# Two layers of dilated local attention and a bilinear GLU: own places for the first chunks' q, k and v, wo loaded directly, and an order planned from other durations

## The chip, the cores and the metric

The kernel runs on one core of a Trainium2 chip. The metric is device time in microseconds of the whole program on that core, so lower is better. The engines have the names of the profile: PE is the matrix engine (TensorE; PEld is its weight load), DVE is VectorE, ACT is ScalarE, POOL is GpSimd, and SP is SyncE, which only issues DMAs here. Everything between them is ordered by semaphores, and each engine works through its own list in order.

## The reference

```python
def _A_ref(x, wqkv, wo):                       # B, S, D = 1, 2048, 576
    H = 32; Dh = D // H                        # 18 values a head
    W, dil = 8, 2
    q, k, v = (x @ wqkv) ...                   # [B, H, S, Dh] each
    idx = pos[:, None] - arange(W) * dil       # the token itself and 7 earlier ones
    logits = einsum("bhsd,bhswd->bhsw", q, k[idx]) * Dh ** -0.5   # -1e9 where idx < 0
    o = einsum("bhsw,bhswd->bhsd", softmax(logits), v[idx])
    return o.reshape(B, S, D) @ wo

def _B_ref(x, w_gate, w_up, w_down):           # F = 4608
    return ((x @ w_gate) * (x @ w_up)) @ w_down

x = x + _A_ref(_layernorm(x), A_wqkv, A_wo)
x = x + _B_ref(_layernorm(x), B_w_gate, B_w_up, B_w_down)
x = x + _A_ref(_layernorm(x), A_wqkv, A_wo)    # the same weights again
x = x + _B_ref(_layernorm(x), B_w_gate, B_w_up, B_w_down)
```

## The kernel before

**Chunks.** The 2048 tokens are 16 tiles of 128. A chunk is one or two tiles that go through one attention and one GLU. There are 18 chunks: first layer pair, tiles 0, 1, 2, 3 one by one (chunks 0 to 3), tiles 4-5 and 6-7 (chunks 4 and 5), second layer pair for tiles 0 to 7 (chunks 6 to 9), then the same for tiles 8 to 15 in pairs (chunks 10 to 17). Chunk 0 is called "fast" in the code and takes shorter ways.

**One attention** (`attention`): `head` makes a layernorm: statistics on DVE (L343, L344), the inverse root as Ln and Exp on ACT (L349, L350), the application on ACT (L358; L359 writes the last 64 columns a second time), and a transpose, on PE through a PSUM bank with a copy on ACT (L369, L372) for chunks 0 to 4, by DMA (L362) for the others. `project` multiplies by `wqkv` on PE (L407) into one pair of PSUM banks after another, and ACT (for chunk 0 partly DVE) moves q, k and v to `qT`, `kT`, `vT` (L460, L477, L484, L449). These have two places, taken in turn by odd and even chunks. k and v have 14 columns of the chunk before in front, the halo, copied by ACT (L392, L453 in, L489 out). DVE multiplies q by two shifts of k at a time (L503) and adds up (L507, L511, L512), PE sums over the head's values with `Esel` (L518), DVE and ACT make the softmax (L540 to L551). The weights are spread over the partitions: for chunks 0 to 4 by four matmuls with `Bsel` (L557), each copied out of PSUM; for the others through `a_dram` in DRAM (L567, L570). DVE multiplies v by them, shift by shift, and adds (L587, L602); PE multiplies by `wo` (L614), DVE adds the residual (L620), and a second `head` gives `xnT_B`, of which there are three.

**One GLU** (`glu`): PE makes 512 columns of gate and up in a pair of PSUM banks (L655, and L666 for the last 64 rows), ACT copies gate (L677), DVE multiplies it by up (L678), and after half of F (a third for a single tile) PE multiplies by `w_down` (L699, L700) and DVE adds into `xf` (L709, L714). `wd` slices of `w_down` come through six buffers, loaded anew for each chunk by SP.

**What sets the order.** All of this is entered as operations of a `Plan`: an engine, a cost in ns, keys read and written, a priority. `Plan.run` takes, at each step and over all engines, the operation that can start earliest by these costs (the priority decides only between equals), and issues it. The result is a fixed list for each engine. A key that is written waits for all earlier readers in the order of entry. `LAT` is added where a result goes to another engine, `margin` where a step on PE waits for another engine. DMA time is counted as bytes at 250 per ns plus 2000 ns. PE's work for attention stands in the same list as the GLU's matmuls.

**The start.** `load_x`, `setup_a`, `setup_b`, `setup_wo` and `setup_glu` enter the loads, all on SP. `wqkv` is put into another order of columns by DVE and ACT (L292, L294). `wo` is copied within DRAM first (L318), then loaded from there (L320, L323). Until chunk 0 is through its attention, its small steps use the third pair of PSUM banks and `acct`; later ones have the one bank `pa`.

Of the kernel before, what the change touches and what calls it, by code (L numbers as in the profile page):

```python
# [15 lines left out]
class Op:  # L16
    __slots__ = ("eng", "cost", "fn", "deps", "order", "succ", "n", "prio", "idx", "hold", "free",
                 "lat", "margin", "ready", "end", "nbytes", "use", "pair", "need")


class Plan:
# [4 lines left out]
    LAT = {"PE": 250, "ACT": 130, "DVE": 110, "POOL": 150, "SP": 0}  # L26
# [6 lines left out]
    def op(self, eng, cost, fn, r=(), w=(), prio=1, after=None, hold=None, free=None, margin=0, nbytes=0, use=None,  # L33
           pair=None, need=None):
        o = Op()
        o.eng, o.cost, o.fn, o.prio, o.hold, o.free = eng, cost, fn, prio, hold, free
# [32 lines left out]
    def run(self, slots):  # L69
        clock = {e: 0.0 for e in self.LAT}  # L70
        dma = 0.0
# [3 lines left out]
        while cand:  # L75
            best = None
            for o in cand:
                t = 0.0
                for p in o.deps:
                    e = p.ready if p.eng != o.eng else p.end  # L80
                    if e > t:
                        t = e
                t += o.margin
                if o.hold is not None:
                    f = free[o.hold]
                    if not f:
                        continue
                    t = max(t, min(f)[0])
                if o.pair is not None:
                    if len(free["unit"]) < len(o.pair):  # L90
                        continue
                    t = max(t, min(free["unit"])[0])
# [21 lines left out]
            if o.nbytes:  # L114
                dma = max(dma, o.end) + o.nbytes / 250.0
                o.ready = dma + 2000
# [16 lines left out]
def kernel(  # L133
# [44 lines left out]
    wo_dram = dram.tile([D, D], BF16, name="wo_dram")  # L178
# [13 lines left out]
    xf = [sb(f"xf{i}", [P, NST, D], FP32) for i in range(NXS)]  # L192
# [9 lines left out]
    xnT_B = [sb(f"xnT_B{i}", [P, KT, CH]) for i in range(NXB)]  # L202
    qT_ = [sb(f"qT{i}", [P, KT, CH]) for i in range(2)]
    kT_ = [sb(f"kT{i}", [P, KT, HALO + CH]) for i in range(2)]
    vT_ = [sb(f"vT{i}", [P, KT, HALO + CH]) for i in range(2)]
    oT = sb("oT", [P, KT, CH])
    n_al = nlayers // 2
    halo_k = [sb(f"halo_k{i}", [P, KT, HALO]) for i in range(n_al)]
    halo_v = [sb(f"halo_v{i}", [P, KT, HALO]) for i in range(n_al)]
# [46 lines left out]
    def load_x(t0, nst):  # L256
        b, i0 = (t0 // 2) % 2, t0 % 2
        op("SP", 600, dma(xb[b][:, i0:i0 + nst, :], xv[:, t0:t0 + nst, :]), w=[f"xb{b}_{i}" for i in range(i0, i0 + nst)],
           nbytes=P * nst * D * 2, prio=1.5 if t0 else 0)
# [13 lines left out]
    def setup_b():  # L273
        def mk_zero():
            for t_ in qT_ + kT_ + vT_:
                nc.gpsimd.memset(t_[TL:P, KF, :], 0.0)
            for t_ in halo_k + halo_v:
                nc.gpsimd.memset(t_[:], 0.0)
        op("POOL", 1500, mk_zero, w=[f"{x}{t}{i}" for x in "qkv" for t in (4, "H") for i in range(2)] + [f"halo{x}{i}" for x in "kv" for i in range(n_al)])
        for k in range(KT):  # L280
            for t3 in (0, 1, 2, 3):
                if t3 < 3:
                    src = wraw[:, k, t3 * D:(t3 + 1) * D].rearrange("p (h d) -> p d h", h=H)[:, 0:16, :]
                    dst = wqkv[:, k, t3 * 512:(t3 + 1) * 512].rearrange("p (d h) -> p d h", h=H)
                    cost = (615, 1080)
                else:
                    src = wraw[:, k, :].rearrange("p (t h d) -> p t d h", t=3, h=H)[:, :, 16:18, :]
                    dst = wqkv[:, k, 3 * 512:3 * D].rearrange("p (t d h) -> p t d h", t=3, h=H)
                    cost = (280, 500)
                rk = [f"wraw{k}"] if k < KF else ["wrawt0", f"wrawt{TL}"]  # L290
                if t3 % 2 == 0:
                    op("DVE", cost[0], lambda dst=dst, src=src: nc.vector.tensor_copy(dst, src), r=rk, w=[f"wq{t3}_{k}"], prio=2)  # L292
                else:
# [10 lines left out]
        op("POOL", 9000, mk_sel, w=["sel"])  # L304
# [12 lines left out]
    def setup_wo():  # L317
        op("SP", 600, dma(wo_dram[:].rearrange("(d h) n -> h d n", h=H), A_wo.rearrange("(h d) n -> h d n", d=Dh)),  # L318
           w=["wod"], nbytes=D * D * 2, prio=2)
        op("SP", 600, lambda: nc.sync.dma_start(wo_p[:, 0:KF, :], wo_dram[0:KF * P, :].rearrange("(t p) n -> p t n", p=P)),  # L320
           r=["wod"], w=["wo0"], nbytes=KF * P * D * 2, prio=2)
        for r_ in (0, TL):
            op("SP", 600, lambda r_=r_: nc.sync.dma_start(wo_p[r_:r_ + TL, KF, :], wo_dram[KF * P:D, :]),  # L323
               r=["wod"], w=[f"wot{r_}"], nbytes=TL * D * 2, prio=2)
# [11 lines left out]
    def head(src, keys, nst, dst, key, prio, ab, on_pe, mg):  # L336

        mv, st, rstd, nmr, xn = mv_[ab], st_[ab], rstd_[ab], nmr_[ab], xn_[ab]
        for i in range(nst):
            def stats(i=i):  # L340
                xr = src(i).rearrange("p (a b) -> p a b", a=2)
                for a in range(2):
                    nc.vector.bn_stats(out=st[:, i, a, :], in_=xr[:, a, :])  # L343
                nc.vector.bn_aggr(out=mv[:, i, :], in_=st[:, i])  # L344
            op("DVE", 1070, stats, r=[keys[i]], w=[f"mv{ab}{i}"], prio=prio)
        mk = [f"mv{ab}{i}" for i in range(nst)]

        def rs():
            nc.scalar.activation(rstd[:, 0:nst], mv[:, 0:nst, 1], ACT.Ln, bias=eps_t[:])  # L349
            nc.scalar.activation(rstd[:, 0:nst], rstd[:, 0:nst], ACT.Exp, scale=-0.5)  # L350
        op("ACT", 490, rs, r=mk + ["eps"], w=[f"rstd{ab}"], prio=prio)
        op("DVE", 210, lambda: nc.vector.scalar_tensor_tensor(nmr[:, 0:nst], mv[:, 0:nst, 0], -1.0, rstd[:, 0:nst],
                                                              op0=ALU.mult, op1=ALU.mult),
           r=mk + [f"rstd{ab}"], w=[f"nmr{ab}"], prio=prio)
        for i in range(nst):
            def apply(i=i):
                x = src(i)
                nc.scalar.activation(xn[i][:, 0:D], x, ACT.Identity, bias=nmr[:, i:i + 1], scale=rstd[:, i:i + 1])  # L358
                nc.scalar.activation(xn[i][:, D:D + TL], x[:, KF * P:D], ACT.Identity, bias=nmr[:, i:i + 1], scale=rstd[:, i:i + 1])  # L359
            op("ACT", 1300, apply, r=[keys[i], f"nmr{ab}", f"rstd{ab}"], w=[f"xn{ab}{i}"], prio=prio)  # L360
            if not on_pe:
                op("SP", 900, lambda i=i: nc.sync.dma_start_transpose(out=dst[:, :, i * P:(i + 1) * P], in_=xn[i][:]),  # L362
                   r=[f"xn{ab}{i}"], w=[key + str(i)], prio=0, nbytes=P * KT * P * 2)
# [3 lines left out]
            def tr(i=i, b=b):  # L367
                for k in range(KT):
                    nc.tensor.transpose(bf(b())[:, k, :], xn[i][:, k * P:(k + 1) * P], ident[:])  # L369
            o = op("PE", 290, tr, r=[f"xn{ab}{i}", "ident"], prio=0, margin=mg, **b.take())  # L370
            pl.also(o, [key + str(i)])
            op("ACT", 700, lambda i=i, b=b: nc.scalar.copy(dst[:, :, i * P:(i + 1) * P], bf(b())), r=[b.key], w=[key + str(i)],  # L372
# [4 lines left out]

    def attention(j, la, t0, nst):
        fast = j == 0
        z = j % 2  # L380
        qT, kT, vT = qT_[z], kT_[z], vT_[z]
# [8 lines left out]
        xk = [f"xA{i}" for i in range(nst)]  # L390
        head(lambda i: xin[:, i0 + i, :], xin_k, nst, xnT_A, "xA", prio, 0, on_pe, mg)
        op("ACT", 250, lambda: nc.scalar.copy(kT[:, :, 0:HALO], halo_k[la][:]), r=[f"halok{la}"], w=[f"kH{z}"], prio=prio)  # L392
# [4 lines left out]
        def project(tag, au, bu, tl, ea, eb, dkeys):  # L397
# [7 lines left out]
            def mm(u, part, k, r_, start, stop):  # L405
                p_, e, c0, m = part
                nc.tensor.matmul(bank(p_, u)[0:m, e * n:(e + 1) * n], lhsT=wqkv[r_, k, c0:c0 + m], rhs=xnT_A[r_, k, 0:n],  # L407
# [45 lines left out]
        op("ACT", 250, lambda: nc.scalar.copy(vT[:, :, 0:HALO], halo_v[la][:]), r=[f"halov{la}"], w=[f"vH{z}"], prio=prio)  # L453
        mpb = 4 // nst
        if nst == 2:
# [3 lines left out]
            def ev_q(m):  # L459
                return (600, lambda u, d: nc.scalar.mul(qT[:, 2 * m:2 * m + 2, 0:n], grp(0, u, 2), qscale), [f"q{2 * m}{z}"], 0)  # L460

            def ev_k(m):
                return (590, lambda u, d: cp(d, kT[:, 2 * m:2 * m + 2, HALO:HALO + n], grp(1, u, 2)), [f"k{2 * m}{z}"], 0)

            project("q", un[0], un[1], tq, [ev_q(0), ev_k(0)], [ev_q(1), ev_k(1)], [f"{x}{z}" for x in ("q0", "k0", "q2", "k2")])
# [3 lines left out]
            tb, vs = 0, slice(0, n)  # L469
        else:  # L470
# [3 lines left out]
            tb, vs = 1, slice(n, 2 * n)  # L474
            tq = [(h_, 0, uq[4 * h_ + e]) for e in range(4) for h_ in range(2)]
            tq += [(0, 1, uv[0]), (1, 1, ut[0]), (0, 1, uv[1]), (1, 1, ut[1]), (0, 1, uv[2]), (0, 1, uv[3])]
        ev_t = [(390, lambda u, d: nc.scalar.mul(qT[0:TL, KF, 0:n], bank(tb, u)[0:TL, 0:n], qscale), [f"q4{z}"], 0),  # L477
                (390, lambda u, d: cp(d, kT[0:TL, KF, HALO:HALO + n], bank(tb, u)[TL:P, 0:n]), [f"k4{z}"], 1),
                (390, lambda u, d: cp(d, vT[0:TL, KF, HALO:HALO + n], bank(1, u)[TL:P, vs]), [f"v4{z}"], 0)]
        if nst == 2:  # L480
            ev_v = [(590, lambda u, d, m=m: cp(d, vT[:, 2 * m:2 * m + 2, HALO:HALO + n], grp(m, u, 2)), [f"v{2 * m}{z}"], 0) for m in range(2)]
            project("v", ut, uv, tv, ev_t, ev_v, [f"{x}{z}" for x in ("v0", "v2", "q4", "k4", "v4")])
        else:
            ev_a = [(600, lambda u, d: nc.scalar.mul(qT[:, 0:KF, 0:n], grp(0, u, 4), qscale), [f"q0{z}", f"q2{z}"], 0),  # L484
                    (590, lambda u, d: cp(d, kT[:, 0:KF, HALO:HALO + n], grp(1, u, 4)), [f"k0{z}", f"k2{z}"], 1)]
# [309 lines left out]
```

## Time and profile before

| | us |
|---|---|
| median of three runs | 1096.06 |
| lowest and highest | 1095.94, 1097.07 |
| the profiled execution, its run | 1094.6 |
| its span in the profile | 1092.5 |
| PE busy | 1057.1 |
| DVE busy | 761.4 |
| ACT busy | 364.1 |
| POOL busy | 5.9 |

The granted clock of PE is 0.991 over the span. The profile lists for each group of instructions its line, engine, operation, tiles, count and mean time; the views by stage give busy time between two moments. Busy times on one engine are of overlapping instructions where they are pipelined, so the time from start to start is the better price of one among many. A few records of matmuls are missing.

### The profile page before, as it was taken

The page shows a single profiled execution, that of the slowest core. Times are in us where ns is not written, and L with a number is a line of the kernel's source. Part 1 is how long each engine was busy: PE and PEld are TensorE (multiplying, and loading weights), DVE is VectorE, ACT ScalarE, POOL GpSimd, SP SyncE. Part 2 cuts the span into 40 slices and gives each one's busy share as a digit, 9 for nine tenths or more (in the row PEclk, how much of TensorE's full clock was granted, in tenths as well). Part 3 has the DMA queues.
Part 4 walks back from the last instruction along what each step waited for, and adds up shares of the span by engine and source line. Part 5 has one row for each costly group of instructions (what it writes and reads, how often), then busy time and mean ns, then how long its engine had stood idle before and what let it go on. Part 6 is the DMA issues. An engine that isn't in the chain of part 4 may idle for free.

```text
span 1092.5 us, 25296 instructions
## 1 busy us (share of the span) xinstructions
PE 1057.1 (97%) x10812; PEld 792.8 (73%) x10812; DVE 761.4 (70%) x1347; ACT 364.1 (33%) x768; POOL 5.9 (1%) x26
## 2 busy tenths in 40 slices
PE   5889999999999999999999899999999999999998
PEld 4668887777777777777767677777787777777775
DVE  6688889697979868798978563785757867322222
ACT  7435254432244443323342222314242232211111
POOL 2000000000000000000000000000000000000000
PEclk9899999999999999999999999999999999999999
DMA  8954563633333532535361434342333323333331
GB/s 261 336 155 119 172 200 98 183 110 97 95 99 102 147 84 74 135 112 155 99 168 24 122 99 122 92 121 56 117 106 122 107 72 121 105 96 109 116 110 55
DMA packets 146239, 133.17 MB, mean 122 GB/s; under 512 B 42000, under 2 KB 145488, under 8 KB 146128
## 3 DMA queue, kind: packets, MB, share of 16 engines
q1 hardware_dynamic: 146128, 131.57, 41.9%
q8 instruction: 84, 1.38, 0.5%
q14 instruction: 27, 0.22, 0.1%
HBM read 118.96 MB, written 4.73 MB: 113 GB/s over the span
## 4 chain that ended last, share of the span: by engine, by line
PE 88%; DVE 5%; DMA 4%; SPq 1%; issue 1%; ACT 1%; DVEq 0%; ACTq 0%
PE pu L655 21%; PE pg L655 21%; PE pg L699 12%; PE pu L699 10%; PE pg L666 6%; PE pg L407 6%; PE pu L407 4%; PE pa L614 3%; PE acct L700 3%; DMA a_dram<-s 2%; DMA ab<-a_dram 1%; SPq L570 1%; DMA wraw<-in_A_wqkv_dram 1%; DVE h L678 1%; DVE prod L503 1%
## 5 line engine op out<-in xcount | busy, mean ns | idle before, releaser
L677 ACT CAST g_sb<-pg 128x512 bf16<-128x512 f32 x288 | 158.9, 586 | 493.6 <-PE pu L666 359.7
L655 PE MATMUL pg<-xnT_B,wg 128*128 128x256 bf16 (+1 forms) x2592 | 301.1, 262 | 1.1 <-ACT xnT_B L372 1.1
L655 PE MATMUL pu<-xnT_B,wu 128*128 128x256 bf16 (+1 forms) x2592 | 301.9, 262 | 0.1
L678 DVE TENSOR_TENSOR h<-pu,g_sb 128x512 bf16<-128x512 f32 x288 | 193.3, 684 | 130.6 <-ACT g_sb L677 74.8
L655 PEld LDWEIGHTS <-wu 128*128 128x128 bf16 x2592 | 225.2, 98 | 40.1 <-issue 16.5
L655 PEld LDWEIGHTS <-wg 128*128 128x128 bf16 x2592 | 230.2, 98 | 28.9 <-issue 1.5
L699 PE MATMUL pg<-wd,h 128*128 128x512 bf16 x648 | 231.9, 382 | 0.0
L700 PE MATMUL acct<-wd,h 128*128 128x64 bf16 x1152 | 222.4, 193 | 0.0
L699 PEld LDWEIGHTS <-h 128*128 128x128 bf16 x1152 | 113.0, 98 | 130.5 <-issue 1.1
L699 PE MATMUL pu<-wd,h 128*128 128x512 bf16 x504 | 191.5, 380 | 0.9 <-DVE h L678 0.9
L587 DVE TENSOR_TENSOR prod<-vT,ab 128x1280 bf16<-128x1280 bf16 (+1 forms) x127 | 94.0, 741 | 47.1 <-DMA ab<-a_dram 46.0
L407 PEld LDWEIGHTS <-wqkv 128*128 128x128 bf16 (+1 forms) x1260 | 98.7, 99 | 25.6 <-issue 14.5
L700 PEld LDWEIGHTS <-h 128*128 128x128 bf16 x1152 | 113.1, 98 | 2.1 <-issue 1.1
L503 DVE TENSOR_TENSOR prod<-qT,kT 128x2560 bf16<-128x2560 bf16 (+1 forms) x72 | 95.7, 1332 | 22.4 <-ACT kT L449 21.9
L602 DVE TENSOR_TENSOR oT<-oT,prod 128x1280 bf16<-128x1280 bf16 (+1 forms) x119 | 90.8, 763 | 3.2
L666 PE MATMUL pu<-xnT_B,wgu_t 64*128 64x256 bf16 (+1 forms) x648 | 79.7, 259 | 4.2 <-DVE h L678 4.2
L407 PE MATMUL pg<-xnT_A,wqkv 128*128 128x256 bf16 (+3 forms) x650 | 79.7, 265 | 2.5 <-ACT xnT_A L372 1.6
L666 PE MATMUL pg<-xnT_B,wgu_t 64*128 64x256 bf16 (+1 forms) x648 | 79.8, 259 | 0.0
L407 PE MATMUL pu<-xnT_A,wqkv 128*128 128x256 bf16 (+3 forms) x610 | 77.2, 266 | 0.1
L709 DVE TENSOR_TENSOR xf<-pg,xf 128x512 f32<-128x512 f32 (+1 forms) x40 | 27.4, 684 | 66.3 <-PE pg L699 58.4
L666 PEld LDWEIGHTS <-wgu_t 64*128 64x128 bf16 x1296 | 50.3, 94 | 27.8 <-issue 22.6
L614 PE MATMUL pa<-wo_p,oT 128*128 128x288 bf16 x310 | 48.2, 286 | 2.5 <-DVE oT L602 1.8
(91 smaller groups left out, 614.0 us busy)
## 6 DMA issues: line engine op xcount, KB each, us to landing
wd<-in_B_w_down_dram SPq DMA_DIRECT2D x324, 288.0 KB, 3.4
ab<-a_dram SPq DMA_DIRECT2D x52, 128.0 KB, 2.7
wg<-in_B_w_gate_dram SPq DMA_DIRECT2D x6, 768.0 KB, 9.4
wu<-in_B_w_up_dram SPq DMA_DIRECT2D x6, 768.0 KB, 10.7
out_dram<-xf SPq DMA_DIRECT2D x8, 288.0 KB, 5.4
wraw<-in_A_wqkv_dram SPq DMA_DIRECT2D x4, 432.0 KB, 5.5
xb<-in_A_x_dram SPq DMA_DIRECT2D x6, 288.0 KB, 4.6
a_dram<-s SPq DMA_DIRECT2D x13, 128.0 KB, 2.2
```

Of the source, the lines that this page charges most:

```text
L407: nc.tensor.matmul(bank(p_, u)[0:m, e * n:(e + 1) * n], lhsT=wqkv[r_, k, c0:c0 + m], rhs=xnT_A[r_, k, 0:n], start=start, stop=stop, skip_g ...
L503: nc.vector.tensor_tensor(late["prod"][p_ % 2][:, :, :, 0:n], q2, k2, op=ALU.mult)
L587: nc.vector.tensor_tensor(js(dst), js(vT[:, :, o0:o0 + n]), abw, op=ALU.mult)
L602: op("DVE", 60 + 3 * n, lambda i_=i_: nc.vector.tensor_tensor(oT[:, :, 0:n], oT[:, :, 0:n], late["prod"][i_ % 2][:, 0, :, 0:n], op=ALU.add ...
L614: nc.tensor.matmul(b()[:, 0:HD], lhsT=oT[:, t, i * P:(i + 1) * P], rhs=wo_p[:, t, hh * HD:(hh + 1) * HD], start=(t == 0), stop=(t == KT - 1))
L655: nc.tensor.matmul(pt[:, e * n:(e + 1) * n], lhsT=w_[:, k, ft * P:(ft + 1) * P], rhs=xT[:, k, 0:n], start=(first and k == 0 and e == 0), s ...
L666: nc.tensor.matmul(ps[:, e * n:(e + 1) * n], lhsT=wgu_t[r_, ft * P:(ft + 1) * P], rhs=xT[r_, KF, 0:n], start=(first and e == 0), stop=not ...
L677: op("ACT", 590, lambda: nc.scalar.copy(g_sb[gs][:, 0:ul], pg[use["slot"]][:, 0:ul]), r=[f"wg_{j}_{u}"], w=[f"g{gs}"], prio=0)
L678: op("DVE", 690, lambda: nc.vector.tensor_tensor(hb[hs][:, 0:ul], pu[use["slot"]][:, 0:ul], g_sb[gs][:, 0:ul], op=ALU.mult), r=[f"wu_{j}_{ ...
L699: nc.tensor.matmul((pg, pu)[i][use["slot"]][:], lhsT=lhs, rhs=wt[:, e % 2, 0:512], start=first, stop=fin)
L700: nc.tensor.matmul(acct[:, i * TL:(i + 1) * TL], lhsT=lhs, rhs=wt[:, e % 2, 512:D], start=(first and i == 0), stop=fin, skip_group_check=True)
L709: op("DVE", 690, lambda i=i, dst=dst: nc.vector.tensor_tensor(dst[:, 0:512], (pg, pu)[i][use["slot"]][:], xs_f[:, i0 + i, 0:512], op=ALU.add),
```

## The change

It has these parts; all loads stay on SP's queue (`first` is always true).

1. q, k and v of the first five chunks have places of their own: the single tiles are the halves of the two existing places, chunk 4 lies in the part of `xf` that holds tiles 4 to 7 later. `xnT_A` and the layernorm's small tiles are also used by halves. k and v are one tile `kv_`, so the halo takes one copy in and one out.
2. x of tiles 4 and 5 is loaded once more, early, into a half of `xf[1]`, and chunk 4's first layernorm reads it there; it is entered with chunk 3.
3. `wo` is loaded straight from its input, in six DMAs of 32 partitions.
4. The reordering of `wqkv` is shared by DVE, ACT and POOL.
5. For transposes on PE the second application (L359) goes, and the last 64 columns are transposed twice. For single tiles two matmuls with `Bsel` share a bank and one copy. Chunk 0's small k and v evacuations are one.
6. Nearly all costs of the plan have other values, and the plan has new rules: a GLU evacuation that is due goes first if another operation would hold it up by more than `SLACK`; a margin also counts after a bank comes free; the landing of transposes and of the spread weights is put later.

```diff
+SLACK = {"DVE": 500, "ACT": 300}
-    LAT = {"PE": 250, "ACT": 130, "DVE": 110, "POOL": 150, "SP": 0}
+    LAT = {"PE": 250, "ACT": 150, "DVE": 150, "POOL": 150, "SP": 0}
...
-                    t = max(t, min(f)[0])
+                    t = max(t, min(f)[0] + o.margin)
...
+                if o.due and (o.eng not in urgent or key < urgent[o.eng][0]):
+                    urgent[o.eng] = (key, o)
+            o = best[1]
+            if not o.due and o.eng in urgent and urgent[o.eng][0][0] < best[0][0] + o.cost - SLACK[o.eng]:
+                best = urgent[o.eng]
...
-                o.ready = dma + 2000
+                o.ready = dma[o.eng] + 2000 + o.late
...
+    xtmp = xf[1][:, 1].bitcast(BF16).rearrange("p (i d) -> p i d", i=NST)
...
-                if t3 % 2 == 0:
+                if t3 == 0 or t3 == 3:
                     op("DVE", cost[0], ... nc.vector.tensor_copy(dst, src) ...)
+                elif t3 == 2:
+                    op("POOL", 1000, ... nc.gpsimd.tensor_copy(dst, src) ...)
...
-        op("SP", 600, dma(wo_dram[:].rearrange("(d h) n -> h d n", h=H), ...
+        for dd in range(4):
+            op("SP", 470, dma(wo_p[32 * dd:32 * dd + 32, 0:KF, :], wv_[:, dd:16:4, :]), ...)
+        for dd in range(2):
+            op("SP", 470, dma(wo_p[32 * dd:32 * dd + 32, KF, :], wv_[:, 16 + dd, :]), ...)
...
-                op("SP", 900, lambda i=i: nc.sync.dma_start_transpose(...), ... nbytes=P * KT * P * 2)
+                op("SP", 1250, lambda i=i, cs=cs: nc.sync.dma_start_transpose(...), ... late=3000)
...
+    def place(j, nst):
+        if nst == 1:
+            z, h = j // 2, j % 2
+            return [2 * z + h], qT_[z][:, :, h * P:h * P + P], kv_[z][:, :, :, h * (HALO + P):(h + 1) * (HALO + P)], h * P
+        if j == 4:
+            return ["x"], q_x, kv_x, 0
+        z = (j + 1) % 2
+        return [2 * z, 2 * z + 1], qT_[z][:], kv_[z][:, :, :, 0:HALO + CH], 0
...
+        if j == 3:
+            head(lambda i: xtmp[:, i, :], ["xt0", "xt1"], NST, xnT_A, "xA", prio, 0, on_pe, mg)
...
-            op("DVE", 60 + 5.6 * n, l1, ...)          # q times k
+            op("DVE", 70 + 5.2 * n, l1, ...)
-                op("DVE", 60 + 2.45 * n, l2, ...)
-                op("DVE", 120 + 2.8 * n, l3, ...)
+                op("DVE", 82 + 2.02 * n, l2, ...)
+                op("DVE", 276 + 2.02 * n, l3, ...)
...
-            op("DVE", 60 + 3 * n, pv, ..., margin=0 if on_pe or i_ else 800)
+            op("DVE", 70 + 2.63 * n, pv, ...)
...
+        guard = {3: ["xt0", "xt1"], 5: zk_x}.get(j, [])
...
-            op("ACT", 590, ... g_sb ..., prio=0)
-            op("DVE", 690, ... hb ..., prio=0, free="unit", use=use)
+            op("ACT", 490, ... g_sb ..., prio=0, due=True)
+            op("DVE", 605, ... hb ..., prio=0, due=True, free="unit", use=use)
```

In the lines above, `n` is the chunk's number of tokens, 128 or 256.

More of the change, by code (lines that the diff above doesn't have):

```diff
@@ L76, in run @@
             best = None
+            urgent = {}
             for o in cand:
@@ L351, in head @@
[L351 to L354, printed above, removed]
+                    nc.vector.bn_stats(out=st[:, ia + i, a, :], in_=xr[:, a, :])
+                nc.vector.bn_aggr(out=mv[:, ia + i, :], in_=st[:, ia + i])
@@ new lines, in head @@
+            op("DVE", 970, stats, r=[keys[i]], w=[f"mv{ab}{ia + i}"], prio=prio)
+        mk = [f"mv{ab}{ia + i}" for i in range(nst)]
+        nk = [f"nmr{ab}{ia + i}" for i in range(nst)]
+        sl = slice(ia, ia + nst)
+        def rs():
+            nc.scalar.activation(rstd[:, sl], mv[:, sl, 1], ACT.Ln, bias=eps_t[:])
+            nc.scalar.activation(rstd[:, sl], rstd[:, sl], ACT.Exp, scale=-0.5)
+        rk = [f"rstd{ab}{ia + i}" for i in range(nst)]
+        op("ACT", 440, rs, r=mk + ["eps"], w=rk, prio=prio)
@@ L367, in tr @@
             def tr(i=i, b=b):
[L368 to L372, printed above, removed]
+                for k in range(KF):
+                    nc.tensor.transpose(bf(b())[:, k, :], xn[ia + i][:, k * P:(k + 1) * P], ident[:])
+                for r_ in (0, TL):
+                    nc.tensor.transpose(bf(b())[r_:r_ + TL, KF, :], xn[ia + i][:, KF * P:D], ident[:])
+            o = op("PE", 290, tr, r=[f"xn{ab}{ia + i}", "ident"], prio=0, margin=mg, **b.take())
+            pl.also(o, [key + str(ia + i)])
+            op("ACT", 590, lambda i=i, b=b, cs=cs: nc.scalar.copy(dst[:, :, cs], bf(b())), r=[b.key], w=[key + str(ia + i)],
                prio=prio, **b.drop())
@@ L389, in attention, with zk @@
         xin, xin_k = (xs_b, bk) if la == 0 else (xs_f, fk)
[L390 to L392 removed]
+        xk = [f"xA{c0 // P + i}" for i in range(nst)]
+        if j != 4:
+            head(lambda i: xin[:, i0 + i, :], xin_k, nst, xnT_A, "xA", prio, 0, on_pe, mg, c0)
+        def zk(*names):
+            return [f"{x}{z}" for x in names for z in zs]
+        hk = [f"halo{la}"]
+        op("ACT", 150, lambda: nc.scalar.copy(kv[:, :, :, 0:HALO], halo[la][:]), r=hk, w=zk("kH", "vH"), prio=prio)
         def bank(p_, u):
@@ L488, in attention @@
-        for d_, dst, hl in (("k", kT, halo_k), ("v", vT, halo_v)):
-            op("ACT", 250, lambda hl=hl, dst=dst: nc.scalar.copy(hl[la][:], dst[:, :, n:n + HALO]),
-               r=[f"{d_}{t}{z}" for t in range(0, KT, 2)], w=[f"halo{d_}{la}"], prio=prio)
-        qk = [f"{d}{t}{z}" for d in "qk" for t in range(0, KT, 2)] + [f"kH{z}"]
+            ev_t += [(270, lambda u, d: cp(d, kT[0:TL, KF, HALO:HALO + n], bank(0, u)[TL:P, 0:n]), zk("k4"), 1),
+                     (270, lambda u, d: cp(d, vT[0:TL, KF, HALO:HALO + n], bank(1, u)[TL:P, 0:n]), zk("v4"), 0)]
```

202 lines of the change are left out of this document (111 added, 91 removed).

## The prediction

> **What bounds the kernel now.** I read the page first (shares and the chain that ended last), then the busy time by stage, then PE's waits, and last the start in time order on SP, DVE, ACT and PE.
>
> ```profile
> span 1092.5 us, 25296 instructions
> PE 1057.1 (97%) x10812; PEld 792.8 (73%) x10812; DVE 761.4 (70%) x1347; ACT 364.1 (33%) x768; POOL 5.9 (1%) x26
> ...
> PE 88%; DVE 5%; DMA 4%; SPq 1%; issue 1%; ACT 1%; DVEq 0%; ACTq 0%
> ```
>
> PE is the bound: at most 1092.5 - 1057.1 = 35.4 us of its idle time, and what it runs at a lower clock, can be won. The stages (start and end, length, then PE, PEld, DVE, ACT, POOL busy, granted clock, DMA share, GB/s) show where that lies:
>
> ```profile
> 0.00:14.40 14.40, 6.35 (x75) 5.77 (x75) 7.68 (x18) 11.35 (x18) 5.87 (x26) 1.00 0.80 241
> 14.40:43.20 28.80, 18.32 (x271) 13.83 (x272) 22.32 (x61) 17.69 (x50) 0.00 (x0) 0.88 0.99 317
> 43.20:60.00 16.80, 16.80 (x268) 14.76 (x268) 9.18 (x20) 5.27 (x13) 0.00 (x0) 0.90 1.08 320
> 60.00:77.20 17.20, 11.74 (x146) 8.28 (x144) 14.95 (x36) 6.45 (x17) 0.00 (x0) 0.90 0.37 114
> 77.20:200.80 123.60, 123.02 (x1768) 100.14 (x1766) 101.14 (x201) 55.23 (x121) 0.00 (x0) 1.00 0.50 148
> 200.80:600.00 399.20, 398.09 (x3783) 295.66 (x3783) 336.23 (x572) 141.42 (x298) 0.00 (x0) 1.00 0.41 111
> 600.00:700.00 100.00, 95.92 (x884) 69.88 (x883) 52.90 (x87) 26.14 (x53) 0.00 (x0) 0.98 0.35 99
> 700.00:1060.00 360.00, 359.14 (x3377) 264.49 (x3374) 207.73 (x341) 95.59 (x191) 0.00 (x0) 1.00 0.36 106
> ```
>
> PE's idle time is 8.05 us up to 14.4 (first projection), 10.48 from there to 43.2 (chunk 0's GLU begins), 0 and 5.46 to 77.2 (chunk 1's GLU begins), 0.58 to 200.8, 6.05 in all from 200.8 to 1060, and 4.81 in the last 32.5 us. The first and the last are chains that the change leaves. So the question is 14.4 to 77.2: 15.9 us idle, plus slow matmuls. Those rows (start, length, operation, why it was late):
>
> ```profile
> 19.65 1.89 PE L407 MATMUL pg<-xnT_A,wqkv 128*128 128x128 bf16 x16
> ...
> 43.20 1.87 PE L655 MATMUL pg<-xnT_B,wg 128*128 128x128 bf16 x16 [1.12 <-ACT xnT_B L372]
> ...
> 64.71 0.79 PE L614 MATMUL pa<-wo_p,oT 128*128 128x288 bf16 x5 [1.85 <-DVE oT L602]
> ...
> 73.62 0.21 PE L518 MATMUL pa<-s,Esel 128*32 128x64 bf16 x4 [2.50 <-DVE s L512]
> ```
>
> The same 16 matmuls take 1.06 us when PE has been busy (L407 at 60.91), so each such block after a pause costs 0.8 more. In all about 4 us before 43.2 and 3 us after it (two L655 blocks, and six L699 at 73.8 with 0.48 between starts instead of 0.245). What PE waits for there is DVE's chain of chunk 0, then of chunk 1.
>
> **The change, part by part.** Times are of the profiled execution; its run took 1094.6 us for a span of 1092.5, and the median is 1096.06, 1.5 above it. Differences carry over. About 0.2% (2.2 us) is what a measurement can tell from nothing.
>
> *Own places.* Chunk 2's projection had to wait for chunk 0's PV (34.1), chunk 3's for chunk 1's: it ran at 60.9 to 67.5, while DVE made the oT that PE then waited for. With own places, and x of tokens 512 to 767 loaded a second time into a free half of xf, projections 2, 3 and 4 hang only on their layernorms. Line 407 is busy 4.01 us for projection 3 and 7.53 us for projection 4 (93.9 to 102.3). Not all fits before 43.2: each needs two of the PSUM pairs, and some 2.1 us of ACT evacuations (0.60, 0.58, 0.27, 0.26, 0.26, 0.59 less overlap) before the next; projections 1 and 2 took from 19.65 to 39.3. I take one more there: -4.5 us with its share of the slow blocks; ends 0 and -10.5 (all that idles). Projection 4 (7.5 us) then covers the 5.46 us before 77.2: -5.5; ends 0 and -5.5. With fewer pauses I take 2 of the 3 us of slow blocks after 43.2: -2; ends 0 and -3.
>
> *What it costs chunk 0's chain.* DVE gets three more groups of statistics before 43.2 (0.81 + 0.21 each), ACT three more applications and copies (0.87 + 0.70), PE blocks of 16 matmuls (0.9 to 1.9) ahead of Esel or gathers. The planner takes what can start earliest, so each can hold a step of chunk 0: at 13.5 to 16.2 two such statistics already hold the kT cast. I take +1.5 us; ends 0 and +4.
>
> *Fewer, larger steps.* One activation less per tile in 12 tiles (0.43 each), two halo copies instead of four per chunk (0.25 each), two broadcasts of 512 instead of four of 256 for the single-tile chunks (each round some 1.1 us on the one pa bank, 51.1 to 54.4): all off PE's path, on ACT with 33% busy. They shorten DVE's chain by 2 us a chunk, and I count them as what lets GLU 1 to 4 follow an earlier GLU 0, not again. PE gains one small transpose per tile: 12 x 0.06, nothing.
>
> *wo directly, order of loads.* SP stands from 7.48 to 15.07 until the detour of wo lands; behind it are all GLU weights, first issued at 16.71. Six loads at 0.5 us take its place, so those come some 6 us earlier. But GLU 0 began when xnT_B was copied, so this is worth 0 while chunk 0's chain sets that point. The second load of x adds one issue, about 0.5 us of SP, behind the weights of wqkv.
>
> *Permutation on POOL.* Five 128x512 strided copies move from DVE to POOL, five 192-wide ones from ACT to DVE. DVE's last copies ran at 12.45 when the data landed. POOL was done at 6.58 and gets about 1.4 us more memsets, so it starts near 8.0. The trace has no copy on POOL: 0.52 us (its 128x512 memset) and 2.2 us (twice ACT's 1.11) bound it. The last copy ends at 12.97 to 19; tails began at 13.64; so 0 to +5.4. I take 1.0, near ACT's row as the same strided read: ends 13.45, cost 0.
>
> The Trainium skill's GPSIMD Engine Reference, section "Performance pitfalls for Q7 kernels", says that a read with a step over 8 bytes runs at some 2.9 cycles an element instead of 1.9; these have 36 bytes. By it a copy is an estimated 1.24 us, and the sum would be 0.6 us longer.
>
> *Waits added.* Chunk 3's residual writes wait for the layernorm that reads the borrowed half, chunk 5's for chunk 4's q, k, v; behind them on DVE stand GLU evacuations, but both readers are at least one GLU (28 us) earlier: 0. A due evacuation makes DVE idle up to 0.9 us ahead of a long product (1.40 - 0.5); DVE is idle 32.3 us between 43.2 and 200.8 and 62.97 to 600, so 0 on PE.
>
> *Handing back.* GLU 4 began at 201.14, just after chunk 4's last xnT_B copy (200.1 + 0.69). To start it 10 us earlier DVE must do its 125 us of 43.2 to 200.8 in 148: 85% instead of 79%. Mostly possible with q, k, v early and the shorter broadcasts: +1.5; ends 0 and +9.
>
> *The new order after 200.8.* Old idle there: 6.05, of which 4.08 is one event at 622 (DVE behind ab, which the a_dram write of 5.39 us delayed). New costs allow 1.2 us more for that read and 3 us more for transposes, but are lower for DVE. I take 0; ends -5 and +21 (second rival).
>
> Sum: -4.5 - 5.5 - 2 + 1.5 + 1.5 = -9.0; median 1096.06 - 9.0 = 1087.
>
> **Rivals.**
> *DVE keeps the pace (0.14).* Chunks 1 to 4 are ready as before, and PE idles at a GLU's start instead. For: 200.8 was just in time. Against: DVE had 20% idle. +6 of the gain is handed back: 1093.
> *The order runs ahead of DVE (0.25): slower.* Planned product, add, two adds for 256 rows fall from 1494 + 687 + 837 to 1401 + 599 + 793 = 2793 ns; in the trace, start to start, they take 1.52 + 0.72 + 0.79 = 3.03. PV pairs: 1486 planned, 1.59 measured. So DVE is 0.95 us late at Esel and 0.85 at wo, against 0.65 allowed: 0.3 + 0.2 per chunk if the lag is paid back between them, up to 1.5 if it is not and evacuations lie behind it. Over 14 chunks 7 to 21 us; it decides above (9.0 + 2.2) / 14 = 0.8 us. At 1.0: 1087 + 14 = 1101. Against: DVE waits 130 us for GLU's results, where a lag is made good.
> *The order doesn't move the projections (0.08).* PSUM pairs and ACT hold them where they are: 1095.
> *More comes of it (0.08).* Half of projection 4 also fits before 43.2, and the 622 event goes: 1087 - 4 - 4 = 1079.
>
> **How the numbers follow.** Forecast 0.45, own range 1081 to 1092. Faster: 0.45 + 0.08 + 0.10 of the first rival + 0.02 of the third = 0.65. Same: 0.10. Slower: 0.25. The range goes from 1079 to 1102; the worse half of the second rival, about 0.13, and some 0.05 below are left out.
>
> **What would show it.** Right: projection 3 on PE before 43, projection 4 before 77; idle of 14.4 to 77 near 5; GLU 0's first L655 between 43 and 46, GLU 1's before 74, GLU 4's near 191; last POOL copy before 14. Wrong: PE waiting on DVE s or oT above 0.8 us per chunk after 200; GLU 0 after 47; a new wait of PE for xnT_B at the starts of GLU 1 to 4; new events like that at 622.

## The result, and the profile after

The changed kernel takes 1102.41 us (median of 14 runs, 1097.85 to 1106.4) against 1095.99 us for the kernel before in the same runs (1093.75 to 1097.66): 1.0057 times as long, 95% interval 1.0041 to 1.0073. It is slower by about 6 us, where 9 us less was forecast. The profiled execution is one of its quicker ones: 1097.85 us, span 1096.0 us. So the traces account for 3.5 us of the loss and the rest needs a second execution, below.

The page (span, busy time, the chain that ended last):

```profile
span 1096.0 us, 25174 instructions
PE 1056.2 (96%) x10753; PEld 792.2 (72%) x10824; DVE 760.3 (69%) x1346; ACT 352.6 (32%) x704; POOL 13.3 (1%) x30
PE 79%; DVE 14%; DMA 3%; issue 2%; SPq 1%; ACT 1%; DVEq 0%
```

PE's busy time looks like that of before, but this page has 10753 matmuls to 10824 weight loads, and a second execution of the same kernel (below) has 10824 of both. So 71 records of matmuls are missing here, and each leaves a gap of at most 0.11 us that looks like idle time. In the chain DVE went from 5% to 14%. The same eight stretches as before (start and end, length, busy PE, PEld, DVE, ACT, POOL, granted clock, DMA share, GB/s):

```profile
0.00:14.40 14.40, 6.22 (x75) 5.35 (x76) 9.44 (x22) 9.55 (x14) 13.35 (x30) 1.00 0.91 253
14.40:43.20 28.80, 22.59 (x360) 18.64 (x356) 22.29 (x63) 18.73 (x44) 0.00 (x0) 0.88 1.08 331
43.20:60.00 16.80, 16.75 (x233) 13.78 (x232) 8.91 (x20) 10.48 (x23) 0.00 (x0) 1.00 0.62 189
60.00:77.20 17.20, 13.40 (x185) 9.82 (x183) 14.27 (x35) 3.71 (x7) 0.00 (x0) 0.90 0.54 166
77.20:200.80 123.60, 122.89 (x1765) 100.03 (x1774) 106.55 (x211) 47.82 (x97) 0.00 (x0) 1.00 0.56 164
200.80:600.00 399.20, 387.24 (x3631) 287.11 (x3655) 335.08 (x566) 135.84 (x277) 0.00 (x0) 0.99 0.41 107
600.00:700.00 100.00, 97.29 (x884) 70.92 (x890) 43.42 (x75) 25.73 (x51) 0.00 (x0) 0.99 0.35 94
700.00:1060.00 360.00, 358.66 (x3359) 264.59 (x3380) 211.03 (x347) 95.75 (x186) 0.00 (x0) 1.00 0.37 106
```

Length less PE busy is PE's idle time. Up to 200.8 it fell from 24.57 to 18.95 us; from there to 1060 it rose from 6.05 to 16.01, but 3.1 us of that are the small gaps of missing records (0.1 before). The ends of the chunks don't depend on such gaps. The last sum into `xf` of chunk 4's GLU starts at 268.5 before and at 261.6 now; that of the last chunk at 1088.8 before and at 1092.5 now. So the start won 6.9 us and the stretch behind it lost 10.6. Of these some 6.9 are idle time (12.9 us in gaps over 0.11, against 6.0 before), and an estimated 1.7 come from one more period of some 3.4 us at half clock after a stop (two where there was one; the last section has their length). What the remaining 2 us are stays open.

PE's rows at the start and at the four longest stops after 200 (start, length, operation; in brackets how long PE stood and for whom):

```profile
42.98 1.05 PE L709 MATMUL pg<-xnT_B,wg 128*128 128x128 bf16 x16 [0.79 <-ACT xnT_B L399]
72.99 0.61 PE L394 MATMUL pa<-ident,xn 128*128 128x128 bf16 x4 [3.75 <-ACT xn L381]
...
307.07 0.27 PE L720 MATMUL pu<-xnT_B,wgu_t 64*128 64x256 bf16 x1 [2.75 <-DVE h L732]
504.76 0.79 PE L668 MATMUL pa<-wo_p,oT 128*128 128x288 bf16 x5 [2.09 <-DVE oT L655]
597.03 0.27 PE L720 MATMUL pu<-xnT_B,wgu_t 64*128 64x256 bf16 x1 [2.66 <-DVE h L732]
624.21 0.77 PE L668 MATMUL pa<-wo_p,oT 128*128 128x288 bf16 x5 [2.11 <-DVE xf L674]
```

GLU 0 starts as early as before, its first block takes 1.05 us instead of 1.87, and 3.75 us are lost ahead of GLU 1. After 200 there are four stops like the one at 622 of before. Why does PE stand at 307? DVE's row before it, then SP's rows from 283 to 302 (issuing instructions: start, time over all of them, line, what; two more reads into `ab` follow):

```profile
305.59 0.82 DVE L641 TENSOR_TENSOR oT<-kv,ab 128x1280 bf16<-128x1280 bf16 x1 [5.49 <-DMA ab<-a_dram]
```

```profile
283.52 11.83 SPq L741 DMA_DIRECT2D wd<-in_B_w_down_dram  x8
295.40 1.21 SPq L387 DMA_TRANSPOSE xnT_A<-xn  x1
296.70 0.52 SPq L621 DMA_DIRECT2D a_dram<-s  x1
301.20 0.80 SPq L624 DMA_DIRECT2D ab<-a_dram  x2
```

Chunk 7's weights were ready at 290.1 (L601 at 289.45 plus 0.69). Their write to `a_dram` stood on SP behind eight `wd` loads, which left in 11.83 us, 1.48 us each where the plan has 0.55. So the write went out 6.6 us late. DVE waited 5.49 us at the first product, the GLU's `h` (L732) stood behind that product on DVE, and PE behind `h`. SP's own waits between 283 and 297 (in all, times, longest) show that the loads were not slow to issue: three of them were held until the load issued just before had landed.

```profile
SPq L741 <- DMA wd<-in_B_w_down_dram: 8.2, 3, 2.9
```

The stops at 504.76 and 597.03 follow late writes of chunks 11 and 13 (3.0 and 7.7 us after their softmax; 9 loads from 573.57 took 12.91 us). The one at 624.21 is the same with another transfer: the output store, with its rows ready at 613.1, left at 618.32 behind nine loads, and DVE's next residual, which writes that part of `xf`, stood 5.16 us for it. The other ten writes left within 0.2 us.

A stop can cost more than its length. These are the 6 us before, at and after 307 (columns as above; the clock is third from the end):

```profile
300.00:306.00 6.00, 4.31 (x43) 3.44 (x41) 0.51 (x2) 1.17 (x2) 0.00 (x0) 1.00 0.66 144
306.00:312.00 6.00, 4.93 (x31) 3.54 (x30) 5.93 (x9) 0.96 (x2) 0.00 (x0) 0.72 0.12 41
312.00:318.00 6.00, 6.00 (x61) 4.67 (x59) 5.90 (x9) 3.14 (x8) 0.00 (x0) 1.00 0.02 4
```

### The profile page after: what moved, and what is told of

It reads as the page before. It is cut to its first block, busy times and chain, and to the rows that moved or that the text cites. A ratio compares the mean times of both kernels' runs of the same rounds, so it can differ in the third digit from the quotient of the medians.

```text
span 1096.0 us, 25174 instructions
## 1 busy us (share of the span) xinstructions
PE 1056.2 (96%) x10753; PEld 792.2 (72%) x10824; DVE 760.3 (69%) x1346; ACT 352.6 (32%) x704; POOL 13.3 (1%) x30
## 4 chain that ended last, share of the span: by engine, by line
PE 79%; DVE 14%; DMA 3%; issue 2%; SPq 1%; ACT 1%; DVEq 0%
PE pu L709 21%; PE pg L709 21%; PE pg L756 10%; PE pu L756 7%; PE pg L720 6%; PE pg L455 4%; DVE oT L655 3%; PE acct L757 3%; DVE prod L641 3%; PE pa L668 3%; PE pu L455 3%; DVE prod L553 2%; DVE h L732 1%; DMA a_dram<-s 1%; DMA ab<-a_dram 1%
## 5 line engine op out<-in xcount | busy, mean ns | idle before, releaser
L709 PE MATMUL pu<-xnT_B,wu 128*128 128x256 bf16 (+1 forms) x2592 | 302.0, 262 | 0.0
L709 PE MATMUL pg<-xnT_B,wg 128*128 128x256 bf16 (+1 forms) x2592 | 301.0, 262 | 0.8 <-ACT xnT_B L399 0.8
L732 DVE TENSOR_TENSOR h<-pu,g_sb 128x512 bf16<-128x512 f32 x288 | 193.4, 686 | 147.1 <-ACT g_sb L731 95.7
L709 PEld LDWEIGHTS <-wu 128*128 128x128 bf16 x2592 | 224.7, 98 | 40.5 <-issue 16.9
L709 PEld LDWEIGHTS <-wg 128*128 128x128 bf16 x2592 | 229.1, 98 | 29.8 <-issue 1.0
L756 PE MATMUL pg<-wd,h 128*128 128x512 bf16 x602 | 215.6, 382 | 0.0
L756 PE MATMUL pu<-wd,h 128*128 128x512 bf16 x479 | 182.0, 380 | 0.0
L553 DVE TENSOR_TENSOR prod<-qT,kv 128x2560 bf16<-128x2560 bf16 (+1 forms) x68 | 90.0, 1325 | 23.0 <-ACT kv L497 21.9
L641 DVE TENSOR_TENSOR prod<-kv,ab 128x1280 bf16<-128x1280 bf16 (+1 forms) x120 | 88.3, 738 | 2.1 <-PE pg L646 1.9
```

What stands on the lines that cost most here:

```text
L553: nc.vector.tensor_tensor(late["prod"][p_ % 2][:, :, :, 0:n], q2, k2, op=ALU.mult)
L641: nc.vector.tensor_tensor(js(dst), js(vT[:, :, o0:o0 + n]), abw, op=ALU.mult)
L709: nc.tensor.matmul(pt[:, e * n:(e + 1) * n], lhsT=w_[:, k, ft * P:(ft + 1) * P], rhs=xT[:, k, 0:n], start=(first and k == 0 and e == 0), s ...
L732: op("DVE", 605, lambda: nc.vector.tensor_tensor(hb[hs][:, 0:ul], pu[use["slot"]][:, 0:ul], g_sb[gs][:, 0:ul], op=ALU.mult), r=[f"wu_{j}_{ ...
L756: nc.tensor.matmul((pg, pu)[i][use["slot"]][:], lhsT=lhs, rhs=wt[:, e % 2, 0:512], start=first, stop=fin)
```

## The experiments

Two theories. **Q**: the loss is SP's queue; writes and stores stand behind bursts of `wd` loads that the plan prices too low. **C**: the loss is DVE's lower prices for the eight attention steps, by which the order runs ahead of DVE (the second rival). The kernel before ran beside each group of runs on the same chip, and all ratios are to it.

**The bounce on another queue.** The write to `a_dram` and the reads into `ab` go to POOL's queue; the order of all engines stays.

```diff
-lambda: nc.sync.dma_start(dr[:, 0:W * sq], ...)
+lambda: nc.gpsimd.dma_start(dr[:, 0:W * sq], ...)
```

> The changed kernel with the five DMAs of the spread softmax weights (a_dram written, ab read back) issued by POOL instead of SP; the plan, and with it the order on every other engine, is the changed kernel's. Theory Q (the queue): after 200 us the changed kernel loses its time where the a_dram write stands on SP behind a burst of wd loads, which leave SP in pairs every 3.8 us although the plan gives each 0.55; DVE then stands at the first product with ab (5.4 us at 305 and at 595), GLU evacuations stand behind it, PE stops, and its clock is 0.72 for 6 us afterwards. Then the three late writes (6.6, 3.0 and 7.7 us after the softmax) go out within 1.5 us, the stops near 307, 505 and 597 fall from 2.7, 2.1 and 2.7 us to under 1, only the stop at 624 (a store of the output that stands behind such a burst) stays, and the median is 10 to 14 us below the changed kernel's 1102.4: 1088 to 1092. Theory C (the costs): the plan's lower DVE prices queue PE's attention steps too early; a queue changes nothing of that: 1099 to 1104.

1109.21 us, ratio 1.0144 (1.0112 to 1.0177). Twelve of the 13 writes leave within 0.3 us of their softmax, the other after 0.63. The stop at 597 is gone. Those near 307, 505 and 624 stay (2.73, 2.64 and 2.73 us), and one of 2.00 us comes at 214.85. DVE at chunk 7:

```profile
314.53 0.83 DVE L641 TENSOR_TENSOR oT<-kv,ab 128x1280 bf16<-128x1280 bf16 x1 [5.46 <-DMA ab<-a_dram]
```

Here the write left on time, at 299.40, but the reads, issued from 303.28 to 305.46 while the loads were under way, had all landed only at 314.4. Neither theory's range was met. The write's place on SP made the stop at 597, but another issuing queue is no remedy.

**The loads on another queue.** `wd` of chunks 1 to 17 from POOL; order and prices stay.

```diff
+            if j:
+                q = nc.gpsimd
```

> The changed kernel with the wd loads of all chunks but the first issued by POOL, again with the plan unchanged, so the order on PE, DVE and ACT is the same. Theory Q: SP is free for everything else, so the stop at 624 behind the output's store goes too: 1085 to 1091, unless POOL issues the loads so slowly that PE waits for wd (324 loads over some 1000 us leave 3.1 us for each). Theory C: 1099 to 1104.

1110.04 us, 1.0137 (1.0093 to 1.0181). Again neither range was met. No write is over 1.2 us late, yet PE stops for other transfers:

```profile
159.76 1.89 PE L455 MATMUL pg<-xnT_A,wqkv 128*128 128x256 bf16 x8 [3.01 <-DMA xnT_A<-xn]
```

The median landing of a `wd` load rose from 3.3 to 3.8 us, that of a transpose into `xnT_A` from 2.8 to 5.1. The Trainium skill's DMA: Bandwidth & Descriptors, section "Issuing engines are not separate DMA queues", says that transfers from all engines share the same DMA engines and that spreading them only saves the time of issue. Both runs agree that nothing beyond the issue was saved. That the kernel was 15 to 16 us slower than before is not what the page says, and the runs don't settle why.

**DVE's prices of before**, nothing else:

```diff
-op("DVE", 70 + 5.2 * n, l1, ...)
+op("DVE", 60 + 5.6 * n, l1, ...)
...
-op("DVE", 70 + 2.63 * n, pv, ...)
+op("DVE", 60 + 3 * n, pv, ...)
```

> The changed kernel with the prices of before for DVE's attention steps alone (products, adds, softmax, products with v); everything else of the change stays. Theory C: the slow drift behind the plan (2.5 us from 62 to 262 us) and the waits of PE for oT and for the residual go, and most of the loss with them: 1085 to 1091. Theory Q: the plan still thinks that a wd load takes 0.55 us of SP; how many a_dram writes fall into a burst is a matter of phase, from one as in the kernel before to three or more: 1093 to 1104, and each PE stop above 1.5 us after 200 us has such a write or store, issued over 2 us after the softmax, right before it.

1084.93 us, 0.9924 (0.9901 to 0.9946). PE's stop of 3.75 us ahead of GLU 1 is gone too (1.41 us is left there, and 2.02 us comes at 44.37), and after 200 its waits for `oT` stay at or under 0.47 us. Six writes still leave over 1 us late, and the two chunks whose spread weights land last after their softmax (12: 12.3 us, 17: 16.3 us) have each a stop:

```profile
575.80 0.27 PE L720 MATMUL pu<-xnT_B,wgu_t 64*128 64x256 bf16 x1 [2.82 <-DVE h L732]
...
928.91 0.28 PE L720 MATMUL pu<-xnT_B,wgu_t 64*128 64x256 bf16 x1 [2.88 <-DVE h L732]
```

**One price for the loads**, with the change's DVE prices kept:

```diff
-            op(eng, 550 if first else 1100, ...
+            op(eng, (550 if j == 0 else 1400) if first else 1100, ...
```

> The changed kernel with one price of the plan changed: a wd load of all chunks but the first takes 1400 ns of SP instead of 550. Theory Q: the plan then sees SP occupied, puts the a_dram writes between loads and the products with ab later, so writes leave within 2 us of the softmax or the wait is planned with evacuations ahead of it: at most one stop above 1.5 us after 200 us, 1085 to 1093. Theory C: 1098 to 1104.

1085.85 us, 0.9929 (0.9906 to 0.9951). All 13 writes leave within 0.5 us, and no stop after 200 is over 0.82. The burst that held chunk 7's write now stands behind it in the order. SP's rows there:

```profile
290.70 0.34 SPq L621 DMA_DIRECT2D a_dram<-s  x1
293.24 1.75 SPq L624 DMA_DIRECT2D ab<-a_dram  x4
295.09 2.52 SPq L387 DMA_TRANSPOSE xnT_A<-xn  x2
297.71 4.33 SPq L741 DMA_DIRECT2D wd<-in_B_w_down_dram  x8
```

Here eight loads leave in 4.33 us, 0.54 each. So 1400 is not the cost of a load everywhere, but a price at which the order no longer counts on a burst to be over.

**The same price in the kernel before.**

```diff
-            op("SP", 550, dma(wd[b][:], wd_v[g]), ...
+            op("SP", 550 if j == 0 else 1400, dma(wd[b][:], wd_v[g]), ...
```

> The kernel before with one price changed: a wd load of all chunks but the first takes 1400 ns of SP in the plan instead of 550. Theory Q: its one long stop (4.1 us at 622, after an a_dram write that left 3.9 us late behind a burst of wd loads) goes, and with it the 2 us of slow clock behind it: 1087 to 1091 against 1094 to 1096. Rival: the price only shifts the order and the kernel before has nothing else to win: 1093 to 1098.

1086.33 us, 0.9927 (0.9907 to 0.9948): the stop at 622 goes. The old kernel gains 8 us by it, the new one gained 14 (1.0057 - 0.9929 = 0.0128).

**Both prices**, and the residual writes of chunk 4 also wait until its own q, k and v, which lie in the same part of `xf`, have been read (the guard: `guard = {3: ..., 4: zk_x, 5: zk_x}`).

> The changed kernel with the wd price of 1400 and with the prices of before for DVE's attention steps, and chunk 4's residual writes held until its own q, k and v have been read. If queue and DVE prices are separate causes, the stops behind late writes and the waits of PE for oT, the residual and s are both gone: 1080 to 1084. If the wd price alone had already removed all that mattered, as its profile without a stop over 0.9 us after 200 suggests: 1084 to 1087.

1077.72 us, 0.9852 (0.9834 to 0.9869). The change leaves out a wait that the kernel before had: its `apply` reads only `nmr` in the plan's keys, no longer `rstd`. In the orders of this run, of the one with DVE's prices alone (above) and of the one with a late `ab` (below), ACT starts the root of a third layernorm when only two of the four tiles of the two before it have been applied, and there are two places for `rstd`. So these three runs do the same work, but partly on overwritten numbers. The last version below has the wait again and takes the same time as this run; the other two were not run with it.

**No rule for due evacuations** (`due=False` at both places).

> The changed kernel without the rule that a due GLU evacuation goes first. Theory Q: the rule has no part in SP's queue; writes still fall into bursts: 1094 to 1106, with a late write before each stop over 1.5 us. If the rule is what starves DVE's attention steps (it makes DVE idle ahead of long steps) the stops before wo and at the products with ab shrink: below 1092.

1103.03 us, 1.0077 (1.0052 to 1.0102): the new rule is not the cause. Chunk 7's write is again late by 7.7 us. The three stops over 1.5 us after 200 stand behind bursts, but at other transfers than the write: 3.89 us at 310.03 for a transpose, 2.20 at 530.48 behind a load of x, and 2.77 at 629.93 behind an output store.

**A later landing of `ab` in the plan** (`late=1200` becomes 6000).

> The changed kernel with the read-back of the spread weights planned to land 6000 ns later than its transfer, instead of 1200; wd loads keep 550. Theory Q in two halves: the writes still leave late behind bursts (some of 13 by over 2 us), since SP's order is nearly the same, but the plan now puts GLU evacuations ahead of the first product with ab, so DVE is not blocked and PE doesn't stop there: 1084 to 1091, with lateness of that product under 1 us. If a late write costs PE its time in another way, stops stay: 1096 to 1104.

1084.22 us, 0.9906 (0.9887 to 0.9925). Three writes still leave 3.6 to 9.4 us late, but the order now puts the product later: DVE waits for late weights at one of these chunks alone (7.99 us, chunk 9), and PE stops after 200 for at most 1.2 us. So a late write costs nothing by itself; it costs where an evacuation of the GLU stands behind the product.

**Everything together**: both prices, the guard, and `apply` also reading `rstd`.

```diff
-r=[keys[i], nk[i]], w=[f"xn{ab}{ia + i}"]
+r=[keys[i], nk[i], rk[i]], w=[f"xn{ab}{ia + i}"]
```

> The change's kernel with the price of a wd load at 1400 from chunk 1 on, the DVE prices of the kernel before for the attention's steps, chunk 4's q, k and v places guarded against the residuals that write into them, and the layernorm's application waiting until its rstd is no longer needed by the next one (in the planner's reads). Every run of the change so far named two causes: SP's late writes (worth about 8 us between the run with the DVE prices alone and the one with both) and the DVE prices (about 8 between the run with the wd price alone and the one with both). The last point only fixes an order that this plan is expected to hold nearly everywhere already, so the time stays where the run with both was: 1075 to 1081, no PE stop above 0.8 us after 200 us, all a_dram writes within 0.5 us of their softmax. If the start's gain is not real (rival: the run with both gains from something left out by the overwritten rstd), it comes to 1084 to 1088, where the kernel before is with the wd price alone.

1079.19 us, 0.9855 (0.9832 to 0.9878), 16 us faster than the kernel before. The stages from 200.8 to 1060:

```profile
200.80:600.00 399.20, 399.20 (x3800) 296.38 (x3798) 338.64 (x570) 139.88 (x282) 0.00 (x0) 1.00 0.41 112
600.00:700.00 100.00, 100.00 (x945) 74.77 (x943) 57.93 (x96) 28.14 (x55) 0.00 (x0) 1.00 0.36 106
700.00:1060.00 360.00, 360.00 (x3377) 265.97 (x3375) 202.56 (x333) 95.17 (x185) 0.00 (x0) 1.00 0.37 106
```

The profile shows no idle time of PE there. DVE waits even here once for 6.96 us, for chunk 12's weights, and PE goes on.

**The change's DVE prices in the kernel before**, the eight lines of the third experiment the other way round.

> The kernel before with nothing but the change's DVE prices for the eight attention steps (l1, l2, l3, three softmax steps, product, addition). Theory that the lower prices alone cost 0.5 to 1.5 us a chunk wherever they stand: 1101 to 1115. Theory that they cost by way of the queue: the order shifts by a few tenths of a us per chunk, the time stays within 1091 to 1101, PE stands 0.3 to 0.9 us at oT and res in most chunks, and every stop over 1.5 us after 200 us follows an a_dram write or an output store that left SP over 1 us late.

1117.38 us, 1.0200 (1.0171 to 1.0229): above both ranges. PE's idle time after 200.8 is 22.2 us (6.05 before). Four writes are 1.3 to 7.2 us late (in the kernel before three, by 1.1 to 3.9). All six stops of 1.9 us or more stand behind bursts on SP: three after the late writes of chunks 7, 13 and 15, one for an output store (3.52 us at 636.55), and two for transposes. For the second of these transposes, SP's and PE's rows:

```profile
367.38 11.81 SPq L250 DMA_DIRECT2D wd<-in_B_w_down_dram  x6
379.30 2.52 SPq L362 DMA_TRANSPOSE xnT_A<-xn  x2
```

```profile
383.48 1.03 PE L407 MATMUL pg<-xnT_A,wqkv 128*128 128x256 bf16 x8 [2.24 <-DMA xnT_A<-xn]
```

**The change again.**

> The change as it is, once more, beside the two above on one chip. Its times spread from 1097.9 to 1106.4 so far. Theory that its stops come from the queue's order, which the program fixes: the same chunks' a_dram writes (7, 11, 13) are late again, with stops of 2 us or more near 307, 505, 597 and 624, and 1097 to 1106. Theory that they are a disturbance of that one execution: other chunks, or none, and a time that moves with them.

1099.96 us (1097.47 to 1104.0), 1.0041 (1.0023 to 1.006). The same three writes are late (6.2, 2.1 and 8.3 us), with stops at 309.33 (2.29), 506.09 (1.18), 599.08 (3.49) and 628.55 (3.64): they belong to the order, not to one execution. Its profiled run took 1104.0 us (span 1102.1) and its page has every matmul:

```profile
PE 1062.9 (96%) x10824; PEld 794.2 (72%) x10824; DVE 759.9 (69%) x1346; ACT 352.3 (32%) x704; POOL 13.5 (1%) x30
```

PE's idle time up to 1060 is 34.6 us here and 35.0 in the quicker execution, which looks equal. Without the gaps of at most 0.11 us, which in the quicker one are nearly all those of missing records, it is 34.5 against 31.2. The granted clock is 0.988 against 0.992; from 600 to 606 it was 0.58 against 0.85. Summed over windows of 6 us, the time lost to the clock (length times 1 less the clock) is 11.9 us against 8.5. So of the 6 us between the two about half is longer stops (3.49 us for 2.66 near 597, 3.64 for 2.11 near 624) and about half is how long PE runs slow after them; what makes them differ was not tried.

## Why the prediction was wrong

| order and DVE prices | load at 0.55 | load at 1.40 |
|---|---|---|
| before, its prices | 1 | 0.9927 |
| before, the change's prices | 1.0200 | not run |
| change, its prices | 1.0057 | 0.9929 |
| change, prices of before | 0.9924 | 0.9855 |

The 0.9855 has the guard and the further read. The 0.9924 has neither, so its order is not one to use.

**The step that failed is "The new order after 200.8"**: 0 taken, with ends of -5 and +21. What it measured is +10.6 us in the profiled execution: from chunk 4's last sum to the last chunk's it takes 830.9 us instead of 820.3. Most of it is the four stops (9.6 us, where there was one of 4.08), and after two of the four the matmuls ran slow. I saw the 4.08 us at 622 and the `a_dram` write behind it, but took them for one event with a landing of 5.39 us, and the later landing in the new plan for its remedy. What the runs showed in its place is SP's queue: a small transfer behind a burst of loads that the plan prices too low, and an evacuation behind that transfer. SP's rows would have shown it before the change: nine loads from 597.54 took 12.34 us there. The price of 0.55 us was a fault in both orders, and which transfers fall behind a burst changed with DVE's prices alone.

**The second rival** (the order runs ahead of DVE, 1101) had the outcome and the prices right, and the way wrong; that its 1101 lies so near the measured 1102.41 is partly luck. Its 1.0 us per chunk is not there: the four long stops add up to 9.6 us in the profiled execution and the waits of 0.3 to 1.2 us at `oT` and `xf` to 2.5; the remaining 3.9 us lie in gaps under 0.3 us, 3.1 of them those of missing records. The pace it worked out holds; DVE's rows in a quiet stretch:

```profile
549.67 0.82 DVE L641 TENSOR_TENSOR prod<-kv,ab 128x1280 bf16<-128x1280 bf16 x1
550.52 0.82 DVE L655 TENSOR_TENSOR oT<-oT,prod 128x1280 bf16<-128x1280 bf16 x1
551.26 0.82 DVE L641 TENSOR_TENSOR prod<-kv,ab 128x1280 bf16<-128x1280 bf16 x1
```

A product and an addition take 1.59 us; the change plans 1.49, the old prices 1.66. The old prices left a little time to absorb a wait, the change's lie below the measured pace. With the load's price mended the old prices are worth 0.9929 - 0.9855 = 0.0074, 8 us; without, 15 and 22 us.

**Own places** (-4.5): idle time of 14.4 to 43.2 fell from 10.48 to 6.21, and projection 3 ran before 43 as forecast. **Projection 4 as cover** (-5.5): wrong in its place. Its 7.70 us ran between 43.2 and 60, where PE had no gap; 60 to 77.2 went from 5.46 only to 3.80, because of the one stop ahead of GLU 1. That stop of 3.75 us hangs on DVE's prices: every run with the change's prices on its order has it, the three with those of before don't. They have one of 1.4 us near 77 instead and, ahead of GLU 0, one of some 2 us near 45. **Slow blocks** (-2): the first L709 took 1.05 us instead of 1.87, and the clock of 43.2 to 60 rose from 0.90 to 1.00; that of 60 to 77.2 stayed at 0.90. **Chunk 0's chain** (+1.5): GLU 0 began at 42.98 instead of 43.20, so it cost nothing that the gain did not hide. **Handing back** (+1.5): GLU 4 began at 193.76, 7.4 us earlier than before and not the 10 that were asked; but idle time of 77.2 to 200.8 is 0.71, was 0.58, so nothing was handed back there, and what is missing was lost ahead of GLU 1. **`wo`, fewer steps, added waits** (0): no wait of PE in the rows above names them.

**The copies on POOL** (1.0 us each, 0): they took 1.26 us in the mean.

```profile
L311 POOL COPY wqkv<-wraw 128x512 bf16<-128x512 bf16 x5 | 6.1, 1261 | 0.0
```

The last ended at 14.18, not 13.45, and PE stood 0.49 us for one. The Trainium skill's rule for steps over 8 bytes (GPSIMD Engine Reference, "Performance pitfalls for Q7 kernels") gave 1.24 us and 0.6 us more for the sum. The mean and the end agree with it, the single copies don't: three took 1.09 to 1.11 us, near ACT's row that I went by, and two 1.51. What makes the two slower was not tried.

**The start as a whole** was nearly right in size once the rest was mended: the last version against the old kernel with the same price for loads and the same DVE prices is 0.9855 - 0.9927, or 7.9 us less, for a sum of -9. It is won where the prediction put it: chunk 4's last sum starts at 261.4 against 268.7, and from there both take 813 us. Under the change's own DVE prices with the load at 1.40 only 1.6 us of it show at that point (267.1). So some 8 of the 9 us were there to be had, and SP's queue and DVE's low prices together took them back and 6 more.

## What to carry to other kernels

A planned order is as good as its most optimistic price. Before trusting a new one, set the planned length of every burst on an issuing queue beside the measured one, and see which small transfer stands behind it. An unexplained stop in the old trace is a mechanism with a place and a trigger; ask where else the trigger can fall, not only whether that one event goes. Prices a little under the measured pace (1.49 us for 1.59) leave no room for a wait; prices a little over it (1.66) on the engine that feeds the bound one were worth 8 us here. And count the records before reading idle time: 71 missing ones looked like 3 us of it.

## What was not expected of the hardware

Eight `wd` loads of 288 KB left SP in 11.83 us in one place and in 4.33 in another. In the first, SP stood three times until the load before had landed (8.2 us in all); why not in the second stays open.

Stops of 2.75 and 2.66 us, at 307 and 597, were followed by a lower clock: 0.50 from 308.3 to 311, and 0.72 over the 6 us after 306, which is 3.36 us at half clock if there are only two rates ((6 - 3.36 / 2) / 6 = 0.72). After those of 2.09 and 2.11 us, at 505 and 624, it was 1.00 over 6 us. Length alone does not decide: 2.82 us at 575.80 in the run with DVE's prices alone left the clock at 1.00, and 2.02 us at 313.82 in the one with the change's prices in the kernel before was followed by 0.72. The Trainium skill's TensorE: Matmul & The Clock Gate, section "What's actually happening", gives a window of 3.41 us that runs freely, and half or full rate. The length agrees; that a stop shorter than the window, 2.75 us, was followed by a period at half rate is not what its table says.
